# A recurrence in chunks with a feed-forward layer on one core: operands kept in the tiles that the products read, fewer transfers, and more of the preparation on GpSimd

## The chip, the core and the metric

The kernel runs on one core of a Trainium2 chip. Time is device time in microseconds (us) of one execution; the shown time is the median of three runs. A separate execution was recorded by the hardware profiler, and all rows below come from it.

The engines are named as the profile names them: PE (TensorE, matrix products), PEld (its weight loads), DVE (VectorE), ACT (ScalarE), POOL (GpSimd) and SP (SyncE, which here only issues DMA transfers). Each works through its own instructions in the order in which they stand.

## The reference

`r, k, v, w, a, b` have the shape (4, 8, 768, 40): batch, heads, time, head dimension. Each of the 32 pairs of batch and head has a 40x40 state.

```
for t in range(768):
    y[t]  = r[t] @ state
    Sa    = state @ a[t]
    state = state * w[t][None, :] - outer(Sa, b[t])
    state = state + outer(v[t], k[t])
x   = y, as (4, 768, 320)
xn  = (x - mean(x)) / sqrt(var(x) + 1e-6) * g_ln
out = x + relu(xn @ w_ch1) @ w_ch2          # 320 -> 1280 -> 320
```

All is float32; the two weight matrices come in as 8-byte words, which the kernel turns into pairs of short floats by itself.

## The kernel before, in words

Time is cut into 24 chunks of 32 steps. Within a chunk the steps are turned into matrix products; only the state goes from chunk to chunk. All 32 heads are worked on together, in two halves (partitions 0 to 39 and 64 to 103).

**prep(c)** makes a chunk's operands. Two scans on DVE (L335 `gE`, L339 `qE`) give the running products of the decay `w`, from the start and from the end. `a` is multiplied by `qE` into a tile `aT` (L343), `k` and `b` by `gE` in place in `bk` (L351). Chunks 0 to 3 (`EARLY = 4`) do these two on DVE, later ones on POOL. DMA then copies `aT` into a tile `abd` that is zero outside two diagonal blocks, since the next product takes both halves at once. The product L361 multiplies `bk` with `abd`: half of the result are b's products with a, a triangle of 32x32 per head; the other half are k's products with a. L364 (DVE) puts the sign on and writes both to `gk`. The triangles go by DMA to `d_l` in DRAM, k's products to `d_k`.

**invert(s)** takes two chunks (a slab): it reads the triangles back (`yv<-d_l`), inverts them by 28 short dependent instructions on DVE (L403 and L407 in turn), and writes them to `d_h`. **merge(c)** reads `d_h` into `hv` and finishes the inverse with two products (L428, L439).

**loads(c)** brings a chunk's operands together: `aT` and k's products by DMA into `x2s`, `v` and `r` into `x2`, `x5s`, `vu`; it transposes k and b (L464, ACT copies L469) into one half of `xk` and copies that to the other half by DMA (`xk<-xk`). **chain(c)** goes from state to state: L487 (`x2s` with the state in `x2`), L497, L514, and L521 on DVE, which scales and writes the next state. **post(c)** makes the output: L535, L550, L567 (which reads `r` from its own padded tile `rbd`), L573 on DVE, L584. **norm** (L699 to L725) and **moe** (L753 into the hidden layer with L756 and L758 behind, L737 out of it, L765, store) work on two chunks at a time; these are the dense products.

**weights** turns 22 tiles of weights into their form. Twelve of them take ACT L619 and DVE L626, L627, L630; the other ten have a second pass on ACT (L621) and their last step on POOL (L634) instead of L630. All then go through ACT L668 and POOL L670 (the first two through L651 and L659).

The order of the instructions on each engine is made ahead of time by `Plan.order`: each operation has an engine, an estimate of its time and a key (about the chunk number at which it is due), and the planner plays the engines forward and takes the ready operation of the smallest key. `first` and `go` are names that an operation can be made to wait for. All transfers stand in one queue, SP's; the framework lets a transfer wait until the one eight places ahead of it has landed. Tiles are used in rings: `aT` 3, `bk` 3, `x2s` 2, `gk` 1.

Of the kernel before, what the change touches and what calls it, by code (L numbers as in the profile page):

```python
# [178 lines left out]
def body(ctx, tc, ea, eb, vr, rd, vt, w1, w1x_in, w2, gl, fe, fd, out):  # L179
# [31 lines left out]
    aT = ring(AT, "aT", 528)  # L211

    abd, = ring(1, "abd", 2, 16, C)
    rbd, = ring(1, "rbd", 2, 16, C)
    gk, = ring(1, "gk", 512)
# [9 lines left out]
    x2s = ring(2, "x2s", 2, 528)  # L225
# [31 lines left out]
    def consts():  # L257
# [32 lines left out]
        for i in range(2):  # L290
# [13 lines left out]
            for t, x, us in ((x2s, "x2s", 1.2), (x2, "x2", 1.4), (x5s, "x5s", 1.2), (xk, "xk", 2.7)):  # L304
                names = dict(
                    x2s=two("x2s", i, 4), x2=two("S", i, 4) + two("v", i) + [("u", i)], x5s=two("r", i) + [("z", i)],
                    xk=two("xk0", i) + two("xk1", i, 4) + [("eye", i), ("ST", i)])[x]
# [1 line left out]
                op(eng, us * (1.2 if i == 0 else 1.0), -60 + i, (), names,
                   (lambda t=t, i=i: G.memset(t[i], 0.0)) if i == 0 else (lambda t=t, i=i: A.memzero(t[i])))  # L310
# [10 lines left out]
    def prep(c):  # L321
        i, s, j, k = c % 2, c // SLAB, c % SLAB, c % BK
        kp = c - 3.4
        t, tb, g, q, at = wa[i], bk[k], gE[i], qE[i], aT[c % AT]
# [18 lines left out]
        op(eng, 0.7 * us, kp, W + [("q", i)], A + ([("first",)] if c == 1 else []), lambda: e.tensor_tensor(  # L343
            out=at[R, 0:512].rearrange("p (h t) -> p h t", t=C),
            in0=t[R, 529:1041].rearrange("p (h t) -> p h t", h=16), in1=q[R, :, 1:33], op=ALU.mult))
# [10 lines left out]
        def f(b=b):  # L356
            pg = bank[b.at].rearrange("p (f n t) -> p f n t", f=2, t=C)
            for h in range(8):
                for bb in range(2):
# [1 line left out]
                    mm(pg[64 * bb:64 * bb + 64, :, h], lhsT=tb[R, 64 * p:64 * p + 64], rhs=abd[R, :, p],  # L361
                       start=True, stop=True)
# [1 line left out]
        op("DVE", 0.68, kp + 0.3, [b, "sign"], ["gk"], lambda b=b: nc.vector.tensor_tensor(  # L364
            out=gk.rearrange("p (n t) -> p n t", t=C), in0=bank[b.at].rearrange("p (n t) -> p n t", t=C),
            in1=sign.unsqueeze(1).broadcast_to([128, 16, C]), op=ALU.mult))
# [13 lines left out]
        op("ACT", 0.62, c - 1.8, [("q", i)], ["qc"], lambda: nc.scalar.copy(  # L380
# [6 lines left out]
    def invert(s):  # L387

        n, c0 = 32 * SLAB, SLAB * s
        k0 = c0 - 2.0  # L390
# [6 lines left out]
        for j in range(1, B - 1):  # L397
# [46 lines left out]
    def loads(c):  # L444
        i = c % 2
        at = aT[c % AT]
# [31 lines left out]
    def chain(c):  # L478
        i, o = c % 2, (c + 1) % 2
        b = Bank("A")  # L480

        def f(b=b):
            prh = bank[b.at][:, 0:CH].rearrange("p (h e) -> p h e", e=D)
            for h in range(8):
                for q in range(4):
# [1 line left out]
                    mm(prh[32 * q:32 * q + 32, h], lhsT=x2s[i][RROW[hf], hf, 32 * p:32 * p + 32],  # L487
                       rhs=x2[i][RROW[hf], hf, p], start=True, stop=True)
# [466 lines left out]
```

## Time and profile before

| | us |
|---|---|
| median of 3 runs | 635.86 (632.21 to 636.94) |
| profiled execution, whole | 636.37 |
| its span, first to last instruction | 634.6 |
| PE busy | 537.4 (85%) |
| DVE busy | 446.5 (70%) |
| ACT busy | 323.6 (51%) |
| POOL busy | 117.6 (19%) |

The span lies 1.8 us below the execution's whole time. Shares are means over the span; the first fifth looks quite unlike the rest, so they are read stage by stage below. PE is busy when a product is in it, whether at full clock or not.

### The profile page before, as it was taken

To read this page: it belongs to the slowest core of one execution; us is meant where nothing else is said; L and a number is where in the kernel's file an instruction comes from. 1 tells how busy PE (TensorE), PEld (TensorE's weight loads), DVE (VectorE), ACT (ScalarE), POOL (GpSimd) and SP (SyncE) were. 2 spreads that over 40 slices of the span, in tenths; PEclk is the share of its full clock that TensorE was granted. 3 is DMA by queue.
4 is the path that set the end of the run, shared out by engine and by line. 5 is a ranking of instruction groups with operands and counts; after the bars stand their busy time and mean duration, and the time that the engine had idled before them with its cause. 6 is when DMAs were issued, how large, how long until landed. Compare 5 with 4: busy or idle time off the path is not lost.

```text
span 634.6 us, 35137 instructions
## 1 busy us (share of the span) xinstructions
PE 537.4 (85%) x15610; PEld 489.7 (77%) x15610; DVE 446.5 (70%) x1114; ACT 323.6 (51%) x836; POOL 117.6 (19%) x109
## 2 busy tenths in 40 slices
PE   0714875888959989899989999999789899999995
PEld 0514764777858879889989988888779799888995
DVE  7588699996488695595785885864876845967742
ACT  9726756664434454564455355354256545644421
POOL 9108055612021220120221021021022100000000
PEclk9999975798969999999989999799799999999998
DMA  6666667365654554446556356446445445452200
GB/s 170 160 176 171 158 161 206 78 155 121 158 152 125 139 134 106 127 122 156 141 127 163 92 138 151 102 112 159 108 122 143 113 106 119 117 134 79 88 32 25
DMA packets 132205, 81.63 MB, mean 129 GB/s; under 512 B 102736, under 2 KB 108880, under 8 KB 132048
## 3 DMA queue, kind: packets, MB, share of 16 engines
q1 hardware_dynamic: 132048, 79.32, 48.8%
q8 instruction: 124, 2.03, 1.3%
q14 instruction: 33, 0.27, 0.2%
HBM read 51.64 MB, written 12.58 MB: 101 GB/s over the span
## 4 chain that ended last, share of the span: by engine, by line
PE 57%; DVE 16%; issue 8%; SPq 6%; DMA 6%; ACT 4%; POOL 2%; DVEq 0%; ACTq 0%; POOLq 0%
PE bank L737 15%; PE bank L753 13%; SPq L253 6%; PE bank L514 4%; PE bank L567 4%; DVE ytmp L403 3%; DVE yv L407 3%; PE bank L361 3%; PE bank L550 3%; PE bank L584 2%; PE bank L464 2%; PE bank L487 2%; PE bank L439 2%; PE bank L535 2%; PE bank L497 2%
## 5 line engine op out<-in xcount | busy, mean ns | idle before, releaser
L737 PE MATMUL bank<-w,hh 128*128 128x320 f32 x480 | 120.2, 336 | 0.0
L753 PE MATMUL bank<-xh,w 128*128 128x256 f32 x480 | 109.2, 289 | 2.2 <-DVE hl L758 1.7
L756 ACT ACTIVATE hh<-bank 128x256 fp32r<-128x256 f32 x120 | 46.1, 384 | 125.3 <-PE bank L753 123.1
L758 DVE SCALAR_TENSOR_TENSOR hl<-bank,hh 128x256 fp32r<-128x256 f32 x120 | 50.3, 420 | 68.3 <-ACT hh L756 65.6
L753 PEld LDWEIGHTS bank<-xh,w 128*128 128x128 f32 x480 | 83.8, 192 | 3.4 <-DVE hl L758 2.0
L351 POOL TENSOR_TENSOR bk<-bk,gE 104x1024 f32<-104x1024 f32 x20 | 45.9, 2294 | 217.5 <-DMA bk<-in_eb_dram 140.3
L737 PEld LDWEIGHTS bank<-w,hh 128*128 128x128 f32 x480 | 79.7, 196 | 3.8
L737 PE MATMUL bank<-w,hl 128*128 128x320 f32 x240 | 76.1, 317 | 0.1
L753 PE MATMUL bank<-xl,w 128*128 128x256 f32 x240 | 68.4, 285 | 1.2 <-DVE xl L725 1.2
L361 PE MATMUL bank<-abd,bk 104*64 104x64 f32 x768 | 32.1, 245 | 35.8 <-POOL mask L266 14.7
L403 DVE TENSOR_TENSOR ytmp<-yv 64x28 f32<-64x28 f32 (+6 forms) x168 | 43.2, 257 | 23.3 <-issue 11.1
L469 ACT COPY xk<-bank 64x320 f32<-64x320 f32 x96 | 40.2, 418 | 35.3 <-PE bank L464 30.9
L361 PEld LDWEIGHTS bank<-abd,bk 104*64 104x64 f32 x768 | 28.8, 157 | 38.0 <-POOL mask L266 14.6
L521 DVE TENSOR_TENSOR x<-bank,x2s 40x320 f32<-40x320 f32 x92 | 44.6, 485 | 10.6 <-PE bank L514 8.4
L514 PE MATMUL bank<-x,xk 128*40 128x40 f32 (+1 forms) x1472 | 43.1, 220 | 9.2 <-ACT x L501 6.1
L514 PEld LDWEIGHTS bank<-x,xk 128*40 128x40 f32 (+1 forms) x1472 | 36.8, 133 | 15.4 <-ACT x L501 6.8
L553 ACT COPY xk<-bank 40x320 f32<-40x320 f32 x96 | 40.2, 418 | 15.2 <-PE bank L550 13.8
L407 DVE TENSOR_TENSOR yv<-yv,ytmp 64x28 f32<-64x28 f32 (+6 forms) x168 | 43.5, 259 | 5.8
L737 PEld LDWEIGHTS bank<-w,hl 128*128 128x128 f32 x240 | 46.9, 195 | 0.7 <-DVE hl L758 0.6
L753 PEld LDWEIGHTS bank<-xl,w 128*128 128x128 f32 x240 | 46.2, 193 | 1.5 <-DVE xl L725 1.5
L573 DVE TENSOR_TENSOR x5s<-bank,mask 64x256 f32<-64x256 f32 x96 | 40.5, 422 | 9.0 <-PE bank L567 6.7
L335 DVE TENSOR_TENSOR_SCAN gE<-wa,start 104x528 f32<-104x528 f32 x24 | 30.8, 1283 | 20.8 <-DMA wa<-in_ea_dram 11.8
(122 smaller groups left out, 1046.5 us busy)
## 6 DMA issues: line engine op xcount, KB each, us to landing
wa<-in_ea_dram SPq DMA_DIRECT2D x48, 162.7 KB
bk<-in_eb_dram SPq DMA_DIRECT2D x48, 160.0 KB
xk<-xk SPq DMA_DIRECT2D x48, 160.0 KB
x2s<-aT SPq DMA_DIRECT2D x48, 82.5 KB
wa<-in_ea_dram SPq DMA_DIRECT2D x24, 165.0 KB
rbd<-in_rd_dram SPq DMA_DIRECT2D x48, 80.0 KB
x<-in_vt_dram SPq DMA_DIRECT2D x48, 80.0 KB
abd<-aT SPq DMA_DIRECT2D x48, 80.0 KB
```

The source lines that it names most:

```text
L351: op(eng, 1.25 * us, kp, [("g", i)], K, lambda: e.tensor_tensor(out=kb, in0=kb, in1=g[R, :, 0:C].unsqueeze(2).broadcast_to([104, 16, 2, C] ...
L361: mm(pg[64 * bb:64 * bb + 64, :, h], lhsT=tb[R, 64 * p:64 * p + 64], rhs=abd[R, :, p], start=True, stop=True)
L403: nc.vector.tensor_tensor(out=tv, in0=yb[:, :, j + 1:, j:j + 1].broadcast_to(S), in1=yb[:, :, j:j + 1, 0:j].broadcast_to(S), op=ALU.mult)
L407: nc.vector.tensor_tensor(out=v, in0=v, in1=tv, op=ALU.add)
L469: op("ACT", 0.45, c - 1.2 + 0.1 * bb, [bs[hf]], [X[hf]], lambda b=bs[hf], zs=zs, hf=hf, bb=bb: nc.scalar.copy(out=xk[i][zs, 1, hf, 8 * bb: ...
L514: mm(pst[ROWS[hf], h], lhsT=xk[i][FROW[hf], 1, hf, p], rhs=x2[i][FROW[hf], hf, p], start=True, stop=True)
L521: nc.vector.tensor_tensor(out=x2[o][rs, hf, ps], in0=bank[b.at][rs, 0:CH].rearrange("p (h e) -> p h e", e=D), in1=x2s[o][rs, hf, 512 + 8 * ...
L573: op("DVE", 0.4, c + 0.5, [b, "mask"], [("z", i)], lambda b=b, zs=zs, ps=ps, hf=hf, bb=bb: nc.vector.tensor_tensor(out=x5s[i][zs, hf, 8 * ...
L737: mm(bank_of(po[u])[:, 0:CH], lhsT=l[:, us], rhs=ws[f"w2_{f}"][:, x], start=f == 0 and n == 0, stop=f == 9 and n == 2)
L753: mm(ph, lhsT=l, rhs=r, start=n == 0, stop=n == 7)
L756: yield "ACT", 0.39, [phs[f]], [("hh", f % 2)], lambda f=f: nc.scalar.activation(out=hht[f % 2], in_=bank_of(phs[f])[:, 0:256], func=AF.Re ...
L758: yield "DVE", 0.42, [phs[f], ("hh", f % 2)], [("hl", f % 2)], lambda f=f: nc.vector.scalar_tensor_tensor(out=hlt[f % 2], in0=bank_of(phs[ ...
```

## The change: what it does

1. `aT` and `abd` go. `a` is multiplied straight into `x2s` (two instructions, one for each half), which becomes a ring of four (`XS = 4`), and L361 reads `x2s`. Since L361 needs zeros where k's products will stand, POOL clears those places first (from chunk 4 on), and they are filled after L361, from `gk` by four transfers of 32 KB, not through DRAM. `gk` becomes a ring of two.
2. `rbd` goes: L567 (now L570) reads `r` from `x5s`, whose other rows POOL clears for each chunk first.
3. The second copy of k and b (`xk<-xk`) is made by two POOL copies, not by DMA.
4. `EARLY` is 2: chunks 2 and 3 have `a`, `k` and `b` multiplied on POOL as well.
5. In `weights`, all 22 tiles take three DVE steps; ACT's second pass and POOL's multiplication go for the ten that had them. The three steps are planned one by one.
6. Keys: the chain, merge and post of chunks 0 and 1 and the first inversion get earlier keys (`soon`). Chunk 2's loads wait for `first`, now the sign step of chunk 1; chunk 3's wait for `second`, the end of the first inversion. Line numbers move by a few.

```diff
-EARLY = 4
+EARLY = 2
-AT = 3
+XS = 4
...
+    soon = lambda c: 2.0 if c < SLAB else 0.0
...
-        kp = c - 3.4
+        kp = c - 3.4 - soon(c)
-        after = [("first",)] if 2 <= c < 4 else []
+        after = [("first",)] if c == 2 else [("second",)] if c == 3 else []
...
-        op(eng, 0.7 * us, kp, W + [("q", i)], A + ([("first",)] if c == 1 else []), lambda: e.tensor_tensor(
-            out=at[R, 0:512].rearrange("p (h t) -> p h t", t=C),
-            in0=t[R, 529:1041].rearrange("p (h t) -> p h t", h=16), in1=q[R, :, 1:33], op=ALU.mult))
         for hf, rs in enumerate(ROWS):
-            dma(kp + 0.05, 82, A, [("abd", 0, hf)], abd[rs, hf].rearrange("p h t -> p (h t)"), at[rs, 0:512])
+            if c >= XS:
+                op("POOL", 0.5, kp - 0.3, (), [("x2k", x, 2 * hf), ("x2k", x, 2 * hf + 1)], lambda vs=slice(VROW[hf], VROW[hf] + C), hf=hf: nc.gpsimd.memset(
+                    x2s[x][vs, hf, 0:512], 0.0))
+            op(eng, 0.7 * us, kp, W + [("q", i)], [("x2a", x, hf)], lambda hf=hf, rs=rs: e.tensor_tensor(
+                out=x2s[x][rs, hf, 0:512].rearrange("p (h t) -> p h t", t=C),
+                in0=t[rs, 529:1041].rearrange("p (h t) -> p h t", h=16), in1=q[rs, :, 1:33], op=ALU.mult))
...
-                    mm(pg[64 * bb:64 * bb + 64, :, h], lhsT=tb[R, 64 * p:64 * p + 64], rhs=abd[R, :, p],
+                    mm(pg[64 * bb:64 * bb + 64, :, h], lhsT=tb[R, 64 * p:64 * p + 64], rhs=x2s[x][R, :, 32 * p:32 * p + 32],
...
-        for bb in range(2):
-            dma(kp + 0.4, 66, ["gk"], [("d_k", c, bb)], d_k[c][bb].rearrange("t f n -> t (f n)"), gk[64 * bb:64 * bb + C])
+        for hf in range(2):
+            for bb in range(2):
+                dma(kp + 0.4 + (1.0 if c < 2 else 0.0), 33, [("gk", i)], [("x2k", x, 2 * hf + bb)],
+                    x2s[x][VROW[hf]:VROW[hf] + C, hf, 256 * bb:256 * bb + 256],
+                    gk[i][64 * bb:64 * bb + C, 256 * hf:256 * hf + 256])
...
     def loads(c):
-            dma(c - 1.2, 84, [("aT", c % AT), ("pc", c % AT)], [("x2s", i, hf)], x2s[i][rs, hf], at[rs])
-            dma(c - 1.2, 66, two("d_k", c), [("x2s", i, 2 + hf)],
-                x2s[i][vs, hf, 0:512].rearrange("t (b n) -> t b n", b=2), d_k[c][:, :, hf].rearrange("b t n -> t b n"))
...
-            dma(c - 0.3, 164, [("xk1", i, hf), ("xk1", i, 2 + hf)], [("xk0", i, hf)], xk[i][zs, 0, hf], xk[i][zs, 1, hf])
+            op("POOL", 1.6, c - 0.3, [("xk1", i, hf), ("xk1", i, 2 + hf)], [("xk0", i, hf)], lambda zs=zs, hf=hf: nc.gpsimd.tensor_copy(
+                out=xk[i][zs, 0, hf], in_=xk[i][zs, 1, hf]))
+            op("POOL", 0.5, c - 0.7, (), [("z", i)], lambda zs=zs, hf=hf: nc.gpsimd.memset(x5s[i][zs, hf], 0.0))
...
     def post(c):
-        for hf, rs in enumerate(ROWS):
-            dma(c - 0.6, 82, (), [("rbd", 0, hf)], rbd[rs, hf], rd[c, hf])
-                    mm(pz[64 * bb:64 * bb + 64, :, h], lhsT=vu[i][R, p].rearrange("p x t -> p (x t)"), rhs=rbd[R, :, p],
+                    mm(pz[64 * bb:64 * bb + 64, :, h], lhsT=vu[i][R, p].rearrange("p x t -> p (x t)"), rhs=x5s[i][R, :, p],
...
         def conv(i, key):
-            sel = i >= 2 and (i - 2) % 4 > 1
-                if sel:
-                    nc.scalar.activation(out=hi.bitcast(F32), in_=hi.bitcast(F32), func=AF.Sign)
-            if sel:
-                op("POOL", 0.9, key, [res] + sg, [("ot", mi)], lambda: nc.gpsimd.tensor_tensor(
-                    out=m.bitcast(F32), in0=m.bitcast(F32), in1=hi.bitcast(F32), op=ALU.mult))
+            for n, f in enumerate((
+                    lambda: V.tensor_scalar(out=m, in0=m, scalar1=3, scalar2=None, op0=ALU.logical_shift_left),
+                    lambda: V.scalar_tensor_tensor(
+                        out=m, in0=lo, scalar=29, in1=m, op0=ALU.logical_shift_right, op1=ALU.bitwise_or),
+                    lambda: V.scalar_tensor_tensor(
+                        out=m, in0=hi, scalar=0x80000000, in1=m, op0=ALU.bitwise_and, op1=ALU.bitwise_or))):
+                op("DVE", 0.5 if n else 0.35, key, [res], [("ot", mi)], f)
```

Three places show how this moves instructions. The first is DVE behind chunk 0's operands, before and then changed (scans stand here as SCALAR_TENSOR_TENSOR; the numbers behind names tell tiles apart).

```order
L335 SCALAR_TENSOR_TENSOR gE_79<-wa_74,start_0_71 104x528
L337 RECIPROCAL last_72<-gE_79 104x16
L339 SCALAR_TENSOR_TENSOR qE_81<-wa_74,last_72 104x528
L343 TENSOR_TENSOR aT_83<-wa_74,qE_81 104x512
L351 TENSOR_TENSOR bk_76<-bk_76,gE_79 104x1024
L364 TENSOR_TENSOR gk_87<-bank_144,sign_70 128x512
```

```order
L333 SCALAR_TENSOR_TENSOR gE_79<-wa_74,start_0_71 104x528
L335 RECIPROCAL last_72<-gE_79 104x16
L364 TENSOR_TENSOR gk_82<-bank_143,sign_70 128x512
L337 SCALAR_TENSOR_TENSOR qE_81<-wa_74,last_72 104x528
L345 TENSOR_TENSOR x2s_95<-wa_74,qE_81 40x512 x2
L351 TENSOR_TENSOR bk_76<-bk_76,gE_79 104x1024
```

Chunk 0's sign step (L364) stands ahead of chunk 1's second scan now, and `a` takes two instructions.

The second place is SP's queue from chunk 1's triangles (`d_l`) to the load of the first slab for its inversion (`yv`), before and then changed.

```order
L253 DMA d_l_176<-gk_87 32x16x32 x2
L253 DMA d_k_153<-gk_87 32x512 x2
L253 DMA abd_85<-aT_84 40x512 x2
L253 DMA bk_75<-in_eb_dram 40x1024
L253 DMA wa_73<-in_ea_dram 40x1041
L253 DMA yv_89<-d_l_176 64x1024
```

```order
L251 DMA d_l_150<-gk_83 32x16x32 x2
L251 DMA x2s_95<-gk_83 32x256 x4
L251 DMA wa_73<-in_ea_dram 40x1041 x2
L251 DMA yv_85<-d_l_150 64x1024
L251 DMA d_h_162<-d_l_150 1024x1x16
```

The transfers between the two are k's products and one load now; `abd` and the load of a `bk` are gone from there.

The third place is POOL behind its first clearing of tiles, up to the multiplications of chunk 4 (before) and of chunk 2 (changed).

```order
L659 TENSOR_TENSOR w1x<-ot_141,w1x 64x320 x2
L670 TENSOR_TENSOR w_0_0_651<-m_143,w_0_0_651 128x256
L351 TENSOR_TENSOR bk_76<-bk_76,gE_78 104x1024
L659 TENSOR_TENSOR w1x<-ot_142,w1x 64x320 x2
L670 TENSOR_TENSOR w_1_0_699<-ot_141,w_1_0_699 128x256
L634 TENSOR_TENSOR m_143<-m_143,r_1_204 128x320
```

```order
L474 COPY xk_100<-xk_100 64x640 x2
L655 TENSOR_TENSOR w1x<-ot_139,w1x 64x320 x2
L343 MEMSET x2s_94 32x512 x2
L474 COPY xk_101<-xk_101 64x640
L655 TENSOR_TENSOR w1x<-ot_140,w1x 64x320 x2
L351 TENSOR_TENSOR bk_77<-bk_77,gE_78 104x1024
L474 COPY xk_101<-xk_101 64x640
L345 TENSOR_TENSOR x2s_96<-wa_73,qE_80 40x512 x2
```

Copies, clearings and the multiplications of chunk 2 stand among the weights' steps, where only weights' steps and chunk 4's multiplication stood.

More of the change, by code (lines that the diff above doesn't have):

```diff
@@ L210, in body @@
     gE, qE = ring(2, "gE", 16, 33), ring(2, "qE", 16, 33)
[L211 to L215, printed above, removed]
+    gk = ring(2, "gk", 512)
     qc, = ring(1, "qc", 4, 128)
@@ L224, in body @@
     x2 = ring(2, "x2", 2, 16, D)
-    x2s = ring(2, "x2s", 2, 528)
+    x2s = ring(XS, "x2s", 2, 528)
     x5s = ring(2, "x5s", 2, 16, C)
@@ L279, in consts @@
         op("POOL", 0.3, -84, (), ["qm"], lambda: G.memset(qm, 0.0))
-        op("POOL", 1.0, -87, (), two("abd", 0), lambda: G.memset(abd, 0.0))
-        op("ACT", 1.0, -59, (), two("rbd", 0), lambda: A.memzero(rbd))
+        for i in range(XS):
+            op("POOL", 1.0, -87 + i if i < 2 else -45 + i, (), two("x2a", i) + two("x2k", i, 4) + two("x2p", i), lambda i=i: G.memset(x2s[i], 0.0))
         op("POOL", 1.0, -88, (), ["ident"], lambda: make_identity(nc, ident))
@@ L360, in f @@
                     p = 8 * bb + h
-                    mm(pg[64 * bb:64 * bb + 64, :, h], lhsT=tb[R, 64 * p:64 * p + 64], rhs=abd[R, :, p],
+                    mm(pg[64 * bb:64 * bb + 64, :, h], lhsT=tb[R, 64 * p:64 * p + 64], rhs=x2s[x][R, :, 32 * p:32 * p + 32],
                        start=True, stop=True)
-        op("PE", 1.08, kp + 0.3, K + two("abd", 0), [b], f, opens=[b], room=["gk"], recs=32)
-        op("DVE", 0.68, kp + 0.3, [b, "sign"], ["gk"], lambda b=b: nc.vector.tensor_tensor(
-            out=gk.rearrange("p (n t) -> p n t", t=C), in0=bank[b.at].rearrange("p (n t) -> p n t", t=C),
+        op("PE", 1.08, kp + 0.3, K + A, [b], f, opens=[b], room=[("gk", i)], recs=32)
+        op("DVE", 0.68, kp + 0.3, [b, "sign"], [("gk", i)] + ([("first",)] if c == 1 else []), lambda b=b: nc.vector.tensor_tensor(
+            out=gk[i].rearrange("p (n t) -> p n t", t=C), in0=bank[b.at].rearrange("p (n t) -> p n t", t=C),
             in1=sign.unsqueeze(1).broadcast_to([128, 16, C]), op=ALU.mult))
@@ L379, in f @@
                 turn(out=bank[b.at][:, 128 * x:128 * x + 104], in_=qc[R, x], identity=ident[R, R])
[L380 removed]
+        op("ACT", 0.62, c - 1.8, [("q", i)] + go, ["qc"], lambda: nc.scalar.copy(
             out=qc[R].rearrange("p x (b t) -> p x b t", b=4), in_=q[R, :, 1:33].rearrange("p (b x) t -> p x b t", x=4)))
@@ L407, in f @@
                 nc.vector.tensor_tensor(out=v, in0=v, in1=tv, op=ALU.add)
-            op("DVE", 0.6, k0 + 0.02 * j, (), ["y", "ytmp"], f)
+            op("DVE", 0.54, k0 + 0.02 * j, (), ["y", "ytmp"] + ([("second",)] if s == 0 and j == B - 2 else []), f)
         op("ACT", 0.4, k0 + 0.4, (), ["y"], lambda: nc.scalar.copy(
@@ L465, in loads @@
             X = [("xk1", i, 2 * bb + hf) for hf in range(2)]
-            op("PE", 0.4, c - 1.2 + 0.1 * bb, two("bk", c % BK) + ["ident"], bs, f, opens=bs, room=X, recs=16)
+            op("PE", 0.4, c - 1.2 + 0.1 * bb, two("bk", c % BK) + ["ident"] + ([("first",)] if c < 2 else []), bs, f, opens=bs, room=X, recs=16)
             for hf in range(2):
@@ L777, in wilds @@
             ea[c].rearrange("f d n -> (f d) n")[:, 0:528])
-        op("DVE", 0.62, NCH + 10, two("wa", c % 2), ["gk"], lambda: nc.vector.scalar_tensor_tensor(
+        op("DVE", 0.62, NCH + 10, two("wa", c % 2), [("gk", 0)], lambda: nc.vector.scalar_tensor_tensor(
             out=wild[0:2 * D], in0=t.bitcast(U32).rearrange("p (h t) -> p h t", t=33)[:, :, 1:33],
```

90 lines of the change are left out of this document (42 added, 48 removed).

## The prediction

> **What bounds the kernel now.** I read the profile by stages, since its shares over the span mix two different kernels: one that still prepares weights and one that has settled. The windows first (start and end in us, length, busy time and instructions of PE, PEld, DVE, ACT and POOL, granted clock, DMA share, GB/s).
>
> ```profile
> 6.20:36.90 30.70, 15.38 (x272) 12.89 (x272) 21.43 (x26) 23.11 (x57) 11.28 (x18) 1.00 0.65 175
> 36.90:130.50 93.60, 57.38 (x1825) 50.69 (x1825) 80.20 (x187) 57.00 (x143) 41.96 (x40) 0.84 0.61 157
> 130.50:182.00 51.50, 41.66 (x1372) 36.88 (x1370) 35.35 (x95) 23.00 (x59) 8.03 (x5) 0.94 0.57 143
> 182.00:600.00 418.00, 394.84 (x11930) 361.58 (x11931) 295.04 (x777) 208.97 (x555) 51.27 (x29) 0.96 0.49 125
> ```
>
> From 182 us PE is busy 394.84 of 418.00, a share of 0.945: 23 us are idle, and nothing that leaves PE's work alone can save more there. From 130.5 to 182 its share is 0.81, and 9.8 us are idle. From 36.9 to 130.5 PE stands idle for 36 us while DVE is busy 80.20 of 93.60: DVE sets the pace there, with inversions, weights and scans in one line. POOL is busy 41.96 in that stretch and little elsewhere.
>
> So the change is worth something in three places: where the start ends, what the middle stretch loses, and the few holes of the settled stage. Since the order of the work changes, I need a mark at which equal work is done. In the kernel before I take chunk 3's L487; in the changed kernel chunk 2's output product L587 has about the same PE work behind it. Behind the mark both have the same remainder.
>
> ```profile
> 130.68 0.80 PE L487 MATMUL bank<-x,x2s 96*32 96x40 f32 x64
> ```
>
> **The changes ahead of the first inversion.** The early timeline gives each step's start and length.
>
> ```profile
> 14.28 1.23 DVE L351 TENSOR_TENSOR bk<-bk,gE 104x1024 f32<-104x1024 f32 x1
> ...
> 23.48 1.26 DVE L335 TENSOR_TENSOR_SCAN gE<-wa,start 104x528 f32<-104x528 f32 x1 [6.04 <-DMA wa<-in_ea_dram]
> ...
> 25.26 0.69 DVE L364 TENSOR_TENSOR gk<-bank,sign 128x512 f32<-128x512 f32 x1 [0.52 <-PE bank L361]
> ...
> 32.06 0.53 SPq L253 DMA_DIRECT2D yv<-d_l  x1
> ...
> 36.92 0.16 DVE L403 TENSOR_TENSOR ytmp<-yv 64x28 f32<-64x28 f32 x1
> ```
>
> ```profile
> PE bank L361 <- DMA abd<-aT: 14.6, 2, 13.7
> ```
>
> Chunk 1's `bk` is ready at 14.28 + 1.23 = 15.51, but the product that reads it waits for the transfer into `abd` (13.7 us the longest wait), and its sign step comes at 25.26. Without `abd` the path is DVE's: the sign step of chunk 0, now ahead (0.69), the scan (1.26) and `a` in two instructions instead of one (0.69 each, the length of the one, because a half is as long per partition) end near 18.4. A product of 2 us and the sign step bring chunk 1's triangles to 21.3, 4.7 us earlier than 25.26 + 0.69 = 25.95. The issue of `yv`, 6.1 us behind the sign step's end, follows at about 25.3, because the queue between holds fewer transfers. It landed 3.06 us after its issue:
>
> ```profile
> 32.06 3.06 DMA yv<-d_l
> ```
>
> So the data are there at 28.4. The scan of chunk 2, which stands on DVE ahead of the inversion and whose load now waits for chunk 1's sign step, ends near 29.8. **The first inversion starts at 29.8 instead of 36.92.**
>
> **From there to the mark.** DVE's groups between 36.9 and 130.5 (busy us, mean ns of one):
>
> ```profile
> L627 DVE SCALAR_TENSOR_TENSOR ot<-r,ot 128x256 uint32<-128x256 uint32 (+1 forms) x13 | 12.5, 959 | 0.4
> L403 DVE TENSOR_TENSOR ytmp<-yv 64x28 f32<-64x28 f32 (+6 forms) x31 | 7.1, 230 | 1.3 <-issue 0.3
> L407 DVE TENSOR_TENSOR yv<-yv,ytmp 64x28 f32<-64x28 f32 (+6 forms) x30 | 7.0, 233 | 1.0
> ...
> L339 DVE TENSOR_TENSOR_SCAN qE<-wa,last 104x528 f32<-104x528 f32 x3 | 5.4, 1785 | 0.2
> ...
> L630 DVE SCALAR_TENSOR_TENSOR ot<-r,ot 128x256 uint32<-128x256 uint32 x7 | 4.1, 582 | 0.2
> ...
> L630 DVE SCALAR_TENSOR_TENSOR m<-r,m 128x256 uint32<-128x256 uint32 x3 | 2.0, 658 | 0.1
> ...
> L630 DVE SCALAR_TENSOR_TENSOR ot<-rx,ot 128x320 uint32<-128x320 uint32 x1 | 0.5, 492 | 0.0
> ```
>
> The changed order has on DVE, from the first inversion to the mark: three whole inversions, 84 short instructions where 61 ran, 23 x 0.24 = +5.5; 5 scans `qE` for 3, 2 x 1.26 = +2.5; one more sign step, +0.7; 20 third weight steps for 7 + 3 + 1 = 11, 9 x 0.49 = +4.4. Against it stand one `bk` less (-1.2), one tile's first two weight steps (-0.9) and one chunk's residual, norm and hidden step (about 3 us in ten small instructions of the same view). Net +8.0, so 88.2 us of work.
>
> A stall comes on top. POOL's removed steps and the ones that it has already are these (the whole page):
>
> ```profile
> L351 POOL TENSOR_TENSOR bk<-bk,gE 104x1024 f32<-104x1024 f32 x20 | 45.9, 2294 | 217.5 <-DMA bk<-in_eb_dram 140.3 <-DMA hv<-d_h 26.4 <-PE bank L720 20.1
> L343 POOL TENSOR_TENSOR aT<-wa,qE 104x512 f32<-104x512 f32 x20 | 24.6, 1231 | 106.6 <-DVE qE L339 53.5 <-DMA x2s<-aT 15.7 <-DMA x2s<-d_k 14.8
> ...
> L634 POOL TENSOR_TENSOR ot<-ot,r 128x320 f32<-128x320 f32 x6 | 5.3, 877 | 5.5 <-ACT qm L430 2.8 <-ACT ot L644 1.6 <-ACT w L668 1.1
> L634 POOL TENSOR_TENSOR m<-m,r 128x320 f32<-128x320 f32 x4 | 4.5, 1134 | 12.8 <-issue 12.8
> ...
> L303 POOL MEMSET vu<- 128x1024 f32 x2 | 1.9, 960 | 0.1
> ```
>
> The weights' ten multiplications go (5.3 + 4.5 = 9.8). Chunks 2 and 3 bring 2 x (2.29 + 2 x 1.23) = 9.5. No row shows a copy on POOL. A copy of 640 elements lies between the clearing's rate (0.60 us) and the multiplication's (1.43 us); I take 1.1, nearer the multiplication because the copy reads as well, and eight of them by the mark are 8.8. So POOL reads SBUF for about 8.5 us more: 50.5 for 41.96. What that does to DVE shows where a multiplication on POOL and a short one on DVE meet:
>
> ```profile
> 134.13 2.18 POOL L351 TENSOR_TENSOR bk<-bk,gE 104x1024 f32<-104x1024 f32 x1 [10.92 <-DMA bk<-in_eb_dram]
> ...
> 134.22 2.21 DVE L407 TENSOR_TENSOR yv<-yv,ytmp 64x108 f32<-64x108 f32 x1
> ```
>
> ```profile
> 11.06 2.24 POOL L310 MEMSET xk<- 128x2560 f32 x1
> ...
> 12.38 1.26 DVE L339 TENSOR_TENSOR_SCAN qE<-wa,last 104x528 f32<-104x528 f32 x1
> ```
>
> The short instruction took 2.21 us for a usual 0.23 and ended with POOL's; the scan beside a clearing took its 1.26. The Trainium skill, SBUF — State Buffer, section Who interferes with whom, has this as a rule: a VectorE instruction with two SBUF inputs contends with a GpSimd instruction that reads SBUF, not with one that only writes, and the one that comes second is fully blocked. Both pairs of rows agree; the rule speaks against this change's copies and multiplications, and for its clearings.
>
> In the stretch, L627 lost 13 x (0.96 - 0.49) = 6.1 and L339 3 x (1.79 - 1.26) = 1.6 in this way, 7.7 us for 42 us of POOL, a share of 0.18 at the least. For 8.5 more us of POOL the price lies between 0.18 x 8.5 = 1.5 and 8.5; no row is nearer to one end, so I take the middle, **5**. Idle time of DVE was 13.4; some 190 gaps of 30 ns, 5.6 us, stay, and of the other 7.8 I keep half, because the chain of earlier chunks now has a lead: 9.5.
>
> The mark then falls at 29.8 + 88.2 + 5 + 9.5 = 132.5, against 130.7: **+1.8**. All of the 7 us won at the beginning are spent again on DVE. The bounds are 29.8 + 88.2 + 1.5 + 9.5 = 129 and 29.8 + 88.2 + 8.5 + 13.4 = 139.9, or -1.7 to +9.2. ACT, which loses ten passes, was busy 57.00 of 93.60 there and counts for nothing.
>
> **The middle stretch.**
>
> ```profile
> 160.03 1.19 POOL L343 TENSOR_TENSOR aT<-wa,qE 104x512 f32<-104x512 f32 x1 [2.12 <-DMA x2s<-aT]
> ...
> 175.99 1.27 POOL L343 TENSOR_TENSOR aT<-wa,qE 104x512 f32<-104x512 f32 x1 [14.76 <-DMA x2s<-d_k]
> ...
> 182.07 0.64 ACT L409 COPY yv<-yv 64x256 f32<-64x256 f32 x1 [4.04 <-DVE yv L407]
> ```
>
> ```profile
> 169.34 4.15 DMA yv<-d_l
> ```
>
> ```profile
> PE bank L514 <- ACT x L501: 6.1, 3, 4.8
> ```
>
> Here SP's one queue sets the pace: POOL's `a` waits for transfers `x2s<-aT` and `x2s<-d_k`, the load of `yv` lands at 173.5, the inversion ends at 182, and PE waits up to 4.8 us behind it. The change takes these transfers away (`xk<-xk`, `x2s<-aT`, `abd`, `rbd`, and two hops through `d_k`: 288 transfers go, 96 small ones come). If the stretch then runs at the settled share, its 41.66 us of PE take 41.66 / 0.945 = 44.1: **-7.4**. The bounds are 0, if the inversion is late for another reason, and -9.8, all of its idle time.
>
> **The settled stage.** Added on POOL for each chunk: two copies (2.2), four clearings of 512 elements (4 x 0.48), `a` by halves (+1.2). With 3.5 now that is near 9 of some 20 us, and none of it waits in the way of a product as long as DVE keeps its 30% of idle time; the stalls that it brings, 0.18 x 3.4 = 0.6 us a chunk, lie in that. Were that cover gone, 20 chunks would cost 12 us. On the other side stands a hole such as this one:
>
> ```profile
> 440.00:460.00 20.00, 16.11 (x415) 14.66 (x413) 15.28 (x46) 6.16 (x16) 2.59 (x2) 0.83 0.46 116
> ```
>
> ```profile
> 439.14 1.27 DMA x2s<-aT
> ```
>
> The chain of waits enters it through a transfer that no longer exists, and PE idles 3.9 us in it. I take half, **-2**, between 0 and -3.9.
>
> **The sum** against the profiled execution of 636.37 us (half a microsecond above the median shown): +1.8 - 7.4 - 2 = -7.6, **629 us**. Its own range, from the bounds, is 622 to 638 (636.4 - 1.7 - 9.8 - 3.9 = 621 at the very best, 636.4 + 9.2 - 7.4 = 638 with the mark late).
>
> **Rivals.**
> *DVE is held by POOL.* The place is the start; the price is set by the share of POOL's time in which DVE stands. If it is half of 50.5 us and not 0.18, 25 - 7.7 = 17.5 us are added instead of 5: the mark is at 145, +14.3, the middle stretch still lacks inversions and regains nothing, and with -2 the time is 636.4 + 14.3 - 2 = 649. For it speak the rows at 134 and the packed DVE; against it that half of POOL's steps before met one-input instructions or nothing. It decides from a mark of about 140 on, where it eats what the middle gives. By the Trainium skill's rule above (SBUF — State Buffer, Who interferes with whom) every meeting of two-input and reading instructions is paid in full, which is this case.
> *The transfers were hidden anyway.* Then the middle and the settled stage give nothing, because DVE's own order makes the inversions late, and 636.4 + 1.8 = 638. For it: PE's waits name DVE and ACT more often than DMA. Against it: 14.76 us of POOL's wait.
> *The shorter path counts fully.* Few collisions (1.5), idle time only in the gaps (5.6): mark at 125, -5.6; with -9.8 and -3.9 it is 617. For it: the first three chains come earlier; against it: DVE has never been that dense.
>
> **How the numbers follow.** Forecast 0.44, POOL holding DVE 0.22, hidden transfers 0.17, shorter path 0.17. The range runs from 611, a few us beyond the best case, to 649, the middle of the worst. About 1% is what a measurement of this kernel can tell from no change. Half of the forecast's chance, the short path and a little of the hidden one lie below 629.5: faster 0.43. Slower than 642.2 are the second case and the forecast's tail: 0.25. Within: 0.32.
>
> **What would show it.** The first inversion at 29.8; chunk 2's L587 at 132 (bounds 129 to 140); DVE above 90% busy up to there; short inversion steps of 1 to 2 us beside POOL's copies; POOL busy some 235 us in all (24 chunks at near 9, and what is left of the weights); PE's share behind the mark at 0.94 at once. I am wrong if a POOL copy takes much over 1.4 us, if PE waits for a POOL copy or clearing in the settled stage, or if the inversions there begin to wait on POOL.

## The result, and the profile after

The change makes the kernel slightly slower: 641.10 us in the median of four runs (637.92 to 643.86) against 634.29 in four runs of the kernel before, a ratio of 1.012 [1.008, 1.017] (in brackets the 95% interval, here and below); beside further kernels later it was 1.005 [1.000, 1.009]. The forecast was 629 us. One kernel's times scatter by up to 3% from run to run, so only ratios of undisturbed runs of one set are compared.

The windows of the changed kernel by the same stages (columns as before; the first two end and begin at its first inversion).

```profile
6.20:33.00 26.80, 11.22 (x232) 9.54 (x232) 15.96 (x22) 21.51 (x56) 21.26 (x31) 1.00 0.58 153
33.00:130.50 97.50, 54.18 (x1735) 47.52 (x1735) 86.64 (x175) 50.12 (x130) 51.40 (x48) 0.74 0.49 125
130.50:182.00 51.50, 46.63 (x1423) 42.65 (x1423) 44.51 (x114) 24.18 (x66) 23.36 (x25) 0.90 0.35 84
182.00:600.00 418.00, 389.27 (x11998) 354.96 (x11998) 310.72 (x787) 215.28 (x576) 130.88 (x144) 0.98 0.36 88
```

PE's idle time up to 130.5 us is 124.3 - 65.4 = 58.9 (before: 124.3 - 72.8 = 51.5), then 4.9 (9.8) and 28.7 (23.2). The start loses 7, the middle stretch wins 5, and the settled stage, where a gain was expected, loses 5.6. Over the whole span PE is idle 637.0 - 531.3 = 105.7 us; before 97.2. The profiled execution's span is only 2.4 us longer than before, since 6 us of the added idle time are given back by PE's busy time (531.3 for 537.4), at a granted clock of 0.98 for 0.96 in the settled stage. A second profile of the changed kernel has 536.9 busy and 106.6 idle: the idle time repeats there, the busy time doesn't. Idle time scatters too, though: two profiles of one kernel below (parts 1 and 2 alone) have 93.1 and 87.2.

The timeline at the first inversion, at the second, and at the mark:

```profile
31.39 1.40 DVE L333 TENSOR_TENSOR_SCAN gE<-wa,start 104x528 f32<-104x528 f32 x1 [8.66 <-DMA wa<-in_ea_dram]
...
33.04 0.15 DVE L407 TENSOR_TENSOR ytmp<-yv 64x28 f32<-64x28 f32 x1
...
83.88 0.19 DVE L407 TENSOR_TENSOR ytmp<-yv 64x28 f32<-64x28 f32 x1
...
144.41 0.28 PE L587 MATMUL bank<-xk,x5s 128*32 128x40 f32 x8
```

```profile
67.77 0.19 DVE L403 TENSOR_TENSOR ytmp<-yv 64x28 f32<-64x28 f32 x1
```

The last row is the second inversion in the kernel before. In the changed kernel the first inversion starts 4 us earlier than before, the second 16 us later, and the mark, chunk 2's output product, falls at 144.4 where 130.7 was its counterpart. PE's waits over the span:

```profile
PE bank L383 <- ACT qc L384: 40.9, 4, 19.5
PE bank L716 <- DVE xn L708: 10.2, 6, 2.9
```

PE's longest waits are for a transposition of the second scan's result (`qc`, 1.8 us before): it stands next in PE's queue while VectorE is still in the first inversion (19.5 us) or in a run of weights' steps (8.4 us). The second row is the norm of the residual: 7.3 of its 10.2 us fall behind 182 us, where before it was 0.6:

```profile
PE bank L720 <- DVE xn L712: 0.6, 2, 0.3
```

### The profile page after: what moved, and what is told of

Its sections match the earlier page's. It is cut to its first block, busy times and chain, and to the rows that moved or that the text cites. A ratio compares the mean times of both kernels' runs of the same rounds, so it can differ in the third digit from the quotient of the medians.

```text
span 637.0 us, 35015 instructions
## 1 busy us (share of the span) xinstructions
PE 531.3 (83%) x15610; PEld 484.3 (76%) x15610; DVE 469.4 (74%) x1122; ACT 322.6 (51%) x848; POOL 231.9 (36%) x263
## 4 chain that ended last, share of the span: by engine, by line
PE 48%; DVE 29%; issue 8%; DMA 6%; SPq 3%; ACT 3%; POOL 1%; DVEq 0%; ACTq 0%; POOLq 0%
PE bank L749 13%; PE bank L733 12%; DVE ytmp L407 5%; DVE yv L411 5%; SPq L251 3%; PE bank L518 3%; PE bank L570 3%; DVE x L525 3%; DVE x5s L576 2%; DMA wa<-in_ea_dram 2%; PE bank L361 2%; DMA yv<-d_l 2%; DVE gE L333 2%; DVE hl L754 2%; PE bank L540 2%
## 5 line engine op out<-in xcount | busy, mean ns | idle before, releaser
L733 PE MATMUL bank<-w,hh 128*128 128x320 f32 x480 | 117.3, 330 | 0.0
L749 PEld LDWEIGHTS bank<-xh,w 128*128 128x128 f32 x480 | 84.3, 194 | 3.0 <-ACT xh L720 1.0
L733 PEld LDWEIGHTS bank<-w,hh 128*128 128x128 f32 x480 | 78.3, 192 | 3.2
L476 POOL MEMSET x5s<- 64x512 f32 x48 | 25.2, 525 | 149.1 <-PE bank L587 124.4
L407 DVE TENSOR_TENSOR ytmp<-yv 64x28 f32<-64x28 f32 (+6 forms) x168 | 50.4, 300 | 16.3 <-issue 5.4
L345 POOL TENSOR_TENSOR x2s<-wa,qE 40x512 f32<-40x512 f32 x44 | 55.3, 1257 | 13.8 <-DVE qE L337 12.0
L351 POOL TENSOR_TENSOR bk<-bk,gE 104x1024 f32<-104x1024 f32 x22 | 51.9, 2360 | 21.0 <-DMA bk<-in_eb_dram 17.6
L343 POOL MEMSET x2s<- 32x512 f32 x40 | 20.8, 521 | 89.3 <-issue 61.9
L383 PE MATMUL bank<-ident,qc 104*128 104x104 f32 x96 | 16.8, 309 | 42.1 <-ACT qc L384 40.9
L505 ACT COPY x<-bank 32x320 f32<-32x320 f32 x96 | 40.1, 417 | 16.8 <-PE bank L501 15.3
```

Source lines behind the costliest of these rows:

```text
L345: op(eng, 0.7 * us, kp, W + [("q", i)], [("x2a", x, hf)], lambda hf=hf, rs=rs: e.tensor_tensor(out=x2s[x][rs, hf, 0:512].rearrange("p (h t ...
L351: op(eng, 1.25 * us, kp, [("g", i)], K, lambda: e.tensor_tensor(out=kb, in0=kb, in1=g[R, :, 0:C].unsqueeze(2).broadcast_to([104, 16, 2, C] ...
L407: nc.vector.tensor_tensor(out=tv, in0=yb[:, :, j + 1:, j:j + 1].broadcast_to(S), in1=yb[:, :, j:j + 1, 0:j].broadcast_to(S), op=ALU.mult)
L505: op("ACT", 0.44, k, [b], [("u", i)], lambda b=b, qs=qs, hf=hf, bb=bb: nc.scalar.copy(out=x2[i][UROW[hf]:UROW[hf] + C, hf, 8 * bb:8 * bb + 8],
L733: mm(bank_of(po[u])[:, 0:CH], lhsT=l[:, us], rhs=ws[f"w2_{f}"][:, x], start=f == 0 and n == 0, stop=f == 9 and n == 2)
L749: mm(ph, lhsT=l, rhs=r, start=n == 0, stop=n == 7)
```

## The experiments

Set 1 undoes one part of the change at a time. All ratios are to the kernel before, measured in the same set; the sets ran on different chips. "PE idle" below is span less PE's busy time of the profiled execution (97.2 before). Three theories are tested: H (GpSimd's reads hold VectorE), O (VectorE itself has more to do) and K (the new keys and gates make the second inversion late).

**The second copies by transfers again.**

```diff
-            op("POOL", 1.6, c - 0.3, [...], [("xk0", i, hf)], ... nc.gpsimd.tensor_copy(...))
+            dma(c - 0.3, 164, [...], [("xk0", i, hf)], xk[i][zs, 0, hf], xk[i][zs, 1, hf])
```

> The changed kernel with part 3 undone: the second copy of k and b by transfers again, not by GpSimd. In the changed kernel these copies hold GpSimd for 48 x 0.80 = 38 us, about 6 of it before chunk 2's output product at 144.4 us. Theory H (GpSimd's reads hold VectorE in the start, and that is why the start is late): the start gets 3 to 6 us shorter, chunk 2's output product starts before 141, and the time against before falls from +1.2% to about +0.5%. Rival O (the start is late because VectorE has more to do and in another order: weights' steps ahead of scans and inversions): nothing changes by more than 2 us, +1.2%, and 48 more transfers in the one queue may cost a little.

Ratio to before 1.008 [1.003, 1.013]; mark at 142.2 instead of 144.4, last weights' step at 138.7 instead of 140.7, second inversion at 84.3, PE idle 105.5. The start is 2.2 us shorter, less than H expected. The time lies within the spread of the changed kernel: this alone doesn't help.

**The weights as before** (the `conv` of before put back).

```diff
+            sel = i >= 2 and (i - 2) % 4 > 1
-            for n, f in enumerate((shift, or low word, or sign)): op("DVE", 0.5 if n else 0.35, ...)
+            op("DVE", 0.75 if sel else 1.1, ...); if sel: op("POOL", 0.9, ...)
```

> The changed kernel with part 5 undone: ten weight tiles take ScalarE's second pass and GpSimd's multiplication again instead of a third VectorE step. VectorE loses ten steps (10 x 0.49 = 5 us and their stalls), GpSimd gets 9.8 us of reading back, all before about 141 us. Theory O: the start gets 5 to 8 us shorter, the time falls to about +0.2% against before. Theory H: the added reading takes back what the steps gave: within 2 us of the changed kernel, +1.0 to +1.4%.

1.017 [1.011, 1.023], PE idle 115.3, 10 us more than in the changed kernel: slower, and by more than H expected. That VectorE's own ten steps make the start late (O) is not borne out.

**Four early chunks.**

```diff
-EARLY = 2
+EARLY = 4
```

> The changed kernel with part 4 undone: chunks 2 and 3 have a, k and b multiplied on VectorE. GpSimd loses 2 x (2 x 1.26 + 2.36) = 9.8 us of reading in the start, VectorE gets 2 x (2 x 0.69 + 1.22) = 5.2 us of work. Theory H: every us of GpSimd there held VectorE for half to one, so 0 to 5 us are won, +0.4 to +1.2% against before. Theory O: VectorE's line gets 5 us longer, and the time with it: +2.0%.

1.008 [1.003, 1.012], PE idle 105.2: as H had it; O expected +2.0%.

**Keys and gates as before.**

```diff
-    soon = lambda c: 2.0 if c < SLAB else 0.0
+    soon = lambda c: 0.0
-        after = [("first",)] if c == 2 else [("second",)] if c == 3 else []
+        after = [("first",)] if 2 <= c < 4 else []
```

> The changed kernel with part 6 undone: no earlier keys for chunks 0 and 1 and the first inversion, the loads of chunks 2 and 3 wait for chunk 1's multiplication again. Rival K (the new keys put chunk 0's and 1's work and the wait for chunk 2's load in front, and the second inversion and the scans behind it late): the second inversion starts near 68 instead of 84 us, and the time falls to about 0 against before. Theories H and O: the order of the first two chunks is not what costs; the time stays within 3 us of the changed kernel, +0.8 to +1.7%.

The edit also undoes the gates that hold the transpositions of chunks 0 and 1. 1.002 [0.997, 1.007], PE idle 96.9. The second inversion and the mark in its timeline:

```profile
66.82 0.15 DVE L407 TENSOR_TENSOR ytmp<-yv 64x28 f32<-64x28 f32 x1
```

```profile
128.22 1.25 PE L587 MATMUL bank<-xk,x5s 128*32 128x40 f32 x64
```

The keys move the second inversion by 17 us and the mark by 16; 9 us of PE's idle time go with them. So the order was a cost of its own in the rows. In time it is less clear: 1.002 lies under the changed kernel's 1.005 to 1.012, but the intervals of 1.002 and 1.005 overlap. Without the new keys the change is worth nothing, not a gain.

Set 2 separates GpSimd's reads from the order.

**The changed kernel again.**

> The changed kernel itself once more, beside the kernels of this set: +0.8 to +1.7% against before, the start as in its first profile (second inversion near 84 us, chunk 2's output product near 144), PE idle about 106 us in all against 97 of before.

1.005 [1.000, 1.009], PE idle 106.6, second inversion at 83.0, mark at 143.9: the trace repeats; the ratio is at the low end.

**GpSimd only writes.** Same order on every engine; this leaves out most of a, k and b's multiplications and of the copies.

```diff
-                x2s[x][rs, hf, 0:512] = t * q            # GpSimd, likewise bk = bk * gE, xk = copy
+                x2s[x][rs, hf, 0:32] = t * q             # a first part, so that the waits stay
+                memset(x2s[x][rs, hf, 0:512], 0.0)       # twice; bk twice, xk once
```

> The changed kernel with the same order on every engine, but GpSimd's long reads replaced: its multiplications of a, k and b and its copies read and compute only a small first part, so that their waits stay, and then clear the tile for about as long as the whole step took (two clearings for a multiplication, one for a copy). Leaves those products out. Theory H (GpSimd's reads hold VectorE): VectorE's stalls beside these steps go (some 20 us of them up to 144 us), chunk 2's output product moves from 144 to 130 or earlier, PE's waits for the norm's VectorE step behind 182 us go from 7 to 1 to 2 us, and the time falls to -1 to -2% against before. Rival K (what costs is the order and the gate on chunk 3's load): the second inversion still starts near 84, chunk 2's output product after 138, the time stays at +0.5% or above.

0.974 [0.969, 0.978], PE idle 91.8; GpSimd was as busy as ever (240.3 us for 231.9). PE was busy 537.0 us, for 536.9 in the changed kernel of this set, so products with cleared operands were not quicker. The mark:

```profile
133.09 0.36 PE L599 MATMUL bank<-xk,x5s 128*32 128x40 f32 x8
```

The stretch from the first inversion to the mark, in the changed kernel and then in this one (VectorE's is the third busy time, behind PE's two):

```profile
33.00:144.40 111.40, 64.20 (x1972) 56.54 (x1972) 99.40 (x214) 55.16 (x141) 55.10 (x52) 0.72 0.47 120
```

```profile
31.90:133.10 101.20, 63.81 (x1974) 56.48 (x1974) 84.79 (x215) 55.22 (x141) 58.13 (x88) 0.75 0.53 135
```

The same 214 or 215 VectorE instructions take 99.40 us beside GpSimd's reads and 84.79 beside its clearings: 14.6 us held. Over the whole span VectorE is busy 426.6 us for 470.5, 43.8 less with the same 1,122 instructions. In the settled stage VectorE falls from 310.72 us (787 instructions) to 278.64 (764). The norm's small steps there, changed and then with clearings:

```profile
L708 DVE TENSOR_SCALAR xn<-xt,mv,rs 128x320 f32<-128x320 f32 x20 | 15.0, 750 | 0.7
L704 DVE SCALAR_TENSOR_TENSOR e<-r,ve 128x1 f32<-128x1 f32 x20 | 10.9, 543 | 0.7
```

```profile
L720 DVE TENSOR_SCALAR xn<-xt,mv,rs 128x320 f32<-128x320 f32 x19 | 10.2, 536 | 0.7
L716 DVE SCALAR_TENSOR_TENSOR e<-r,ve 128x1 f32<-128x1 f32 x19 | 4.3, 228 | 0.7
```

PE's wait behind `xn` falls from 7.3 to 1.2 us:

```profile
PE bank L728 <- DVE xn L720: 1.2, 1, 1.2
```

Theory H is shown here, with its price: 0.974 / 1.005 in the same set, 3.1%, some 20 us, more than H expected; 14.8 us of it are PE's idle time in the two profiles (91.8 for 106.6). The mark did not get to 130, and the second inversion still stands at 78.7: the order's share remains.

**Only chunk 3's gate moved.**

```diff
-        after = [("first",)] if c == 2 else [("second",)] if c == 3 else []
+        after = [("first",)] if 2 <= c < 4 else []
```

> The changed kernel with one gate moved: chunk 3's loads wait for chunk 1's sign step, as chunk 2's do, not for the end of the first inversion. The new keys stay. Rival K, in the form that the gate is at fault (chunk 3's scan at 52 instead of 30 us, so its triangles and the second inversion come 16 us late): the second inversion starts near 68 us and the time falls to the +0.2% that all keys undone gave. In the form that the keys are at fault: the second inversion stays behind 78, the time above +0.7%. Theory H expects no change.

1.006 [1.001, 1.010], no change. In its profile the second inversion starts at 75.0, between what the two forms of K expected, and the mark still falls at 143.3. The gate by itself is not the cause.

**Parts 1 and 2 alone**: `a` and `r` in the products' tiles, no `aT`, `abd`, `rbd` or `d_k`; all else as before, but for the planner's estimate of an inversion step, which the change also lowered from 0.60 to 0.54 us and which stays at 0.54 here.

```diff
-EARLY = 2
+EARLY = 4
+            dma(c - 0.3, 164, [...], [("xk0", i, hf)], ...)    # copies, conv, soon and gates as before
```

> Parts 1 and 2 alone: a and r in the tiles that the products read, k's products from tile to tile, GpSimd's clearings for it; second copies by transfers, four early chunks, weights and keys as before. 240 of 836 transfers fewer. If the forecast was right that transfers cost the middle stretch 7 us: -1.0% against before. If they were hidden anyway: within 0.4%. If GpSimd's clearings hold VectorE as well: +0.5%.

0.976 [0.971, 0.982], PE idle 93.1: faster than both kernels, and by more than any of the three cases expected (240 transfers go, but 96 small ones come). Its windows:

```profile
6.20:130.50 124.30, 74.17 (x2258) 64.61 (x2260) 111.06 (x222) 80.51 (x206) 72.05 (x81) 0.82 0.59 148
130.50:182.00 51.50, 46.73 (x1482) 42.98 (x1478) 40.82 (x111) 27.43 (x75) 20.38 (x17) 0.90 0.45 105
182.00:600.00 418.00, 392.45 (x11755) 359.64 (x11743) 300.26 (x766) 210.12 (x563) 98.41 (x104) 0.98 0.42 99
```

PE's idle time in the start is 50.1 us for 51.5, and the middle stretch wins 5 us where the forecast gave 7.4 to the removed transfers; the stage behind idles 25.5 (23.2 before). PE's idle time shows 4 us of the 15 us that the ratio gives.

Set 3 adds one part to these two.

```diff
+ copies by GpSimd      (plus_copies)
+ EARLY = 2             (plus_two_early)
+ three VectorE steps   (plus_weights)
+ soon and the gates    (plus_keys)
```

> Parts 1 and 2 (-2.4% against before) with part 3 added: the second copies by GpSimd. Theory H, now that clearings in place of GpSimd's reads gave -2.6%: 38 us more of GpSimd's reads, with VectorE held for some 0.3 of them and PE waiting for part of that: +3 to +8 us on parts 1 and 2, -1.1 to -1.9% against before. If transfers were the price: -2.6% or better, since 48 more go.

0.994 [0.989, 0.999], PE idle 97.5. Its middle stretch idles 4.9 us, as with the two parts alone (4.8); behind 182 us it idles 28.7 for their 25.5, and there PE waits for the norm:

```profile
PE bank L723 <- DVE xn L715: 7.8, 6, 2.4
```

The two parts alone have 4.9 us of this wait (7.5 in one order of set 5), so it does not by itself tell the copies' price. More is lost than H expected.

> Parts 1 and 2 with part 4 added: chunks 2 and 3 multiplied on GpSimd, 9.8 us of its reads in the start for 5.2 us of VectorE. Theory H: +2 to +6 us on parts 1 and 2, -1.4 to -2.1% against before. Theory O (VectorE's own work counts): -2.7 to -3.2%.

1.003 [0.999, 1.007], PE idle 95.5. No theory expected so much: 2.1 to 2.7% lost against the two parts alone, of which PE's idle time shows 2.4 us (95.5 for 93.1). Where the rest is lost is not shown; in this profile PE is busy 544.6 us at a granted clock of 0.929, for 532.9 at 0.939.

> Parts 1 and 2 with part 5 added: all weight tiles by three VectorE steps. VectorE gets ten steps (5 us), GpSimd loses 9.8 us of reads, all in the start. Theory H: within 3 us of parts 1 and 2, rather faster, -2.2 to -2.8%. Theory O: 5 us slower, -1.6%.

0.998 [0.994, 1.003], PE idle 97.4. Neither theory expected this: less reading on GpSimd, 5 us more on VectorE, and 1.6 to 2.2% lost. The rows show 4.3 us of it as idle time, 3.5 of them in the middle stretch, which idles 8.3 us (PE 43.20 of 51.5) where the two parts alone idle 4.8.

> Parts 1 and 2 with part 6 added: the earlier keys and the gates. Rival K: the second inversion moves from 64 to behind 78 us, the start ends 8 to 13 us later, and +5 to +8 us remain, -1.2 to -1.7% against before. Theories H and O: the keys move no work from engine to engine, -2.0 to -2.8%.

1.008 [1.004, 1.013], PE idle 103.1, and the second inversion late, as rival K had it:

```profile
83.23 0.20 DVE L407 TENSOR_TENSOR ytmp<-yv 64x28 f32<-64x28 f32 x1
```

In the two parts alone it starts at 63.8, and PE idles 10.0 us less. The time is worse than K expected, too.

Set 4 prices the reads that were there before, and the copies, each in an unchanged order.

```diff
-        at[R, 0:512] = t * q; bk = bk * gE              # before: GpSimd, chunks 4 to 23
+        at[R, 0:32] = t * q; memset(at[R, 0:512]) twice; likewise bk
```

> The kernel before, in its own order, with its multiplications of a, k and b on GpSimd cut to a small first part and filled up with clearings (leaves those products out). They read for 70 us before, 145 us with the copies after. Theory H, price in proportion: the changed kernel lost 2.0 to 3.9% by its reads, so before loses half of that, and this kernel takes -1.0 to -1.8%; the change's added reads then cost as much again, and its transfers gained about 0.5 to 1%. If the price lies in the order alone, or only above some load of GpSimd: within 0.5%.

0.989 [0.985, 0.993], as H in proportion had it. 70.5 us of reads (45.9 + 24.6) cost before 1.1%; 145.5 (51.9 + 55.3 + 38.3) cost the changed kernel 3.1%. VectorE is busy 428.8 us for 446.5 here: before, the reads held it for 17.7 us, a share of 0.25 of their time; in the changed kernel for 43.8, a share of 0.30. PE's idle time shows little of the 1.1% (95.7 for 97.2), so that price rests on the times.

```diff
-                xk[i][zs, 0, hf] = copy of xk[i][zs, 1, hf]      # changed kernel
+                two of its columns; memset(xk[i][zs, 0, hf], 0.0)
```

> The changed kernel in its own order, with the copies of k and b on GpSimd alone replaced by clearings (leaves the copies out). Of 145 us of reads 38 go. Theory H, in proportion: 0.26 of 2.6 to 3.1%, -0.8% against the changed kernel, about 0 against before. If the copies meet nothing on VectorE: as the changed kernel, +0.5 to +1.2%.

0.998 [0.994, 1.003]: 0.6% under the changed kernel's 1.005 (the intervals overlap), and 1.4% under its 1.012. So the copies' reads cost something near 1%. Set 1 didn't show this; there the copies went to the transfer queue and the order moved with them, which may be why.

> Parts 1 and 2 alone once more: -1.8 to -2.9% against before, if the gain is the kernel's and not that of one set of runs; the stretch from 150 to 200 us is where it is won (10 us).

0.982 [0.976, 0.988]: the gain holds. From 150 to 200 us PE idles 3.0 us for 8.9 before, so 6 us are won there, not 10. PE idles 87.2 in all, 19.2 of it from 182 to 600 us.

Set 5 does the same work in another order.

```diff
-            op("DVE", 0.54, k0 + 0.02 * j, ...)      # inversion step: two_parts_other_plan, changed_other_plan
+            op("DVE", 0.6, k0 + 0.02 * j, ...)
-        op("ACT", 0.62, c - 1.8, ...)                # copy of the scan's result: two_parts_third_plan
+        op("ACT", 0.65, c - 1.8, ...)
```

> Parts 1 and 2, the same instructions, with the planner's estimate of an inversion step at 0.60 us (as before the change) instead of 0.54. If the gain is what parts 1 and 2 do: -1.5 to -2.7% against before. If it hangs on a lucky order: above -1.0%.

0.993 [0.988, 0.997]: 1 to 1.7% lost by the order alone, so the size of the gain hangs on the order. This kernel, with the estimate of before, is parts 1 and 2 and nothing else. Its profile doesn't show where the loss is: PE idles 87.0 us, no more than in the other order.

> Parts 1 and 2, the same instructions, with the planner's estimate of one ScalarE copy (of the scan's result for its transposition) at 0.65 us instead of 0.62, which moves few instructions. If the gain is what parts 1 and 2 do: -1.5 to -2.7% against before. If it hangs on a lucky order: anywhere between -2.5 and +0.5%.

0.979 [0.972, 0.986], 624.12 us in the median, the lowest of all.

> The changed kernel, the same instructions, with the estimate of an inversion step at 0.60 us. If its loss is what its parts do: +0.3 to +1.5% against before. If the order decides: more than 1% away from the changed kernel's +0.5 to +1.2%, to either side.

1.007 [1.002, 1.011], as the changed kernel.

So the two parts gain 0.7 to 2.4% in four measurements and three orders, and the changed kernel loses 0.5 to 1.2% in three and two. A step of 1 to 1.7% between two kernels of different order can be the order; the losses of 1.2 to 3.3% in set 3 are therefore not put down to their parts, except that the keys' late second inversion, with 10 us of idle time, is seen in the rows. Why the weights' part and the two early chunks cost 1.6 to 2.7% stays open.

## Why the prediction was wrong

- **What bounds the stages** was right, and so was the lead ahead of the first inversion in all but its last step: chunk 1's sign step began at 20.75, worked out as 20.6. That it fits so well is partly luck: the sum ran through `a`, which was done at 17.4, but the product waited for `bk`, done at 18.65. The step that failed is chunk 2's scan, and with it the queue: I let 4.0 us pass from the sign step's end to the issue of `yv`, and it took 5.9, nearly the 6.1 of before. I had the scan end near 29.8, so its data by about 28.5; the chain of waits shows

```profile
26.10 5.20 DMA wa<-in_ea_dram
```

  behind four small transfers of k's products, so the data were there at 31.3 and the inversion began at 33.0, 3.2 us late.
- **The mark** was put at 132.5 and fell at 144.4, outside its bounds of 129 to 140. The 11.9 us are 3.2 from the late scan, 6.2 of VectorE's work (99.4 busy for 88.2 + 5) and 2.5 of its idle time (12.0 for 9.5). The number of instructions was nearly right (214 ran; my list makes some 209). The mark was not quite one of equal work: 2,204 products are done by then, 2,098 by its counterpart, and the kernel before had done 2,204 at 133.1, so the changed kernel is 11.3 us late there rather than 13.7. A copy took 0.80 us, not 1.1, and GpSimd was busy 231.9 us for "some 235". The term mis-sized is GpSimd's hold: 7.7 + 5 = 12.7 counted, at least 14.6 measured with the weights' own steps not even replaced. That accounts for 1.9 of the 6.2 us; whether the rest is hold by the weights' steps or work missing from my list is not separated. My share of 0.18 rested on two groups of rows; the other instructions in the line were held too, and over the whole span the share was 0.25 before and 0.30 after.
- **What the order costs** is the step that is missing. I compared the amount of work up to the mark and not when each inversion would be done. Chunk 3's sign step comes at 69.9 in the changed kernel, and the second inversion 14 us behind it; with the old keys (the second row) the sign step comes at 51.8, the second inversion starts 17 us earlier, and the mark is at 128.

```profile
69.85 0.69 DVE L364 TENSOR_TENSOR gk<-bank,sign 128x512 f32<-128x512 f32 x1
```

```profile
51.76 0.68 DVE L364 TENSOR_TENSOR gk<-bank,sign 128x512 f32<-128x512 f32 x1
```

- **The middle stretch** was right: 13.7 us late at the mark, the changed kernel is 2.8 us late at chunk 5's first product (changed, then before):

```profile
177.78 0.32 PE L491 MATMUL bank<-x,x2s 96*32 96x40 f32 x12
```

```profile
174.95 1.14 PE L487 MATMUL bank<-x,x2s 96*32 96x40 f32 x64
```

  That would be 10.9 regained, above the bound of 9.8, but by equal numbers of products (3,289 are done by the first of these two, 3,336 by the second, and the kernel before had done 3,289 at 173.4) it is 11.3 us late at the mark and 4.4 here: 6.9 regained, for 7.4 forecast. PE's idle time in the stretch falls by 5. That the removed transfers did it is borne out by the two parts alone, which win the same 5.
- **The settled stage** was forecast at -2 and idles 5.6 more. The step that failed is "none of it waits in the way of a product as long as DVE keeps its 30% of idle time". DVE was idle 26% of that stage, and PE waited 7.3 us for the norm's chain of small steps, for 0.6 before and 1.2 without the reads: a mean share of idle time did not cover it. How much of the 5.6 this is stays open. In three profiles of the changed kernel's instructions PE idles 28.7, 28.9 and 26.0 us there, for 23.2 before; in four of the two parts alone it idles 19.2 to 25.5, although it waits 3.5 to 7.5 us for the norm in them, and they are the faster kernels. The case "were that cover gone" was priced at 12 us in that very paragraph.
- **The rival "DVE is held by POOL"** was the right mechanism, as the rule of the Trainium skill that it named has it (SBUF — State Buffer, Who interferes with whom). It had the wrong place, the start alone, and so the wrong course: most of what was lost there was regained by 182, where the rival let nothing be regained, and VectorE was held in the settled stage as well (310.7 us for 278.6). GpSimd's reads cost 3.1% after and 1.1% before; the 2.0% between them are 13 us. Without the reads the two kernels stand at 0.974 and 0.989, 1.5% apart in favour of the change (two sets). Put down to the transfers alone, that would be 9.5 us for the 9.4 forecast; but the other parts and the order are in it, so this is not shown. The price of getting it by GpSimd was larger than the gain.

## What to carry to other kernels

Price work moved to GpSimd by what it holds, not by GpSimd's own idle time: replace its reads with clearings of the same length in the same order, which one kernel settles. Take the parts of such a change one by one: here the two that mainly removed transfers gained 0.7 to 2.4% and the whole lost. And where a planner makes the order, measure one part in two or three orders of the same work before a per cent is put down to it.

## What was not expected of the hardware

Not only instructions with two large inputs are held. A shift of a weight tile with one input took 2.08 us for a usual 0.32 beside a multiplication on GpSimd,

```profile
127.59 2.19 POOL L351 TENSOR_TENSOR bk<-bk,gE 104x1024 f32<-104x1024 f32 x1
...
127.89 2.08 DVE L626 TENSOR_SCALAR ot<-ot 128x320 uint32<-128x320 uint32 x1
```

and steps of one element per partition (`e`, 0.23 us in the mean beside clearings) took 0.54 in the mean behind 182 us. The Trainium skill, in the same section, counts a tensor_scalar that runs in a two-port mode among those that contend; the row agrees with that, though no run here shows the mode.
